# Layer two's list scheduler counts the SBUF port that VectorE and GpSimd share, with the output rows due one hidden row later

## The chip, the cores and the metric

One core of one Trainium2 chip runs the whole program. The metric is device time in microseconds, the median of several executions. One further execution was taken by the hardware profiler; all rows below are from it. PE is TensorE, DVE is VectorE, ACT is ScalarE, POOL is GpSimd, SP is the queue that issues most DMAs.

## The reference

Eight batches of eight-head Nystrom attention feed two feed-forward layers, all in fp32.

```python
x = attn_out.transpose(0, 2, 1, 3).reshape(B * S, H * D)   # 4608 x 512
a = x @ w1;  b = x @ w2
y = (a * b) @ w3 @ w_out                                   # layer one
h = y @ w_in                                               # 512 -> 2048
g = np.where(h > 0, h, np.exp(np.minimum(h, 0)) - 1)
out = g @ w_out2                                           # 2048 -> 512
```

## The kernel before

Attention and layer one fill the first part of the span. Every fp32 matrix is split into a high part (cast to fp32r) and a low part (source minus high), and each product is three matmuls: high by high, high by low, low by high.

**Layer two** works on transposed data in five blocks of 768, 1024, 1024, 1024 and 768 tokens. A block is cut into two halves (384 or 512 columns). For each block `i` and each of eight pairs `p` of 128-wide hidden slices there is a unit `u`, forty in all. A unit forms its 2x2 block product with seven multiplications in place of eight: `h_row` (L946) is one of them, a **hidden row** of six matmuls into one of two PSUM banks `h0`, `h1`, taken in turn. `h_put` (L969) empties the bank into the SBUF tile `g`: rows 0, 2, 3 and 6 are copied by ACT (L974), rows 1, 4 and 5 are added to what is there by DVE (L976: one operand in PSUM, one in SBUF). The next hidden row but one writes the same bank, so PE waits for the put.

After a half's puts come the ELU steps: ACT forms `m` and `t` (L987, L991, L995), DVE multiplies (`t<-m,t`, L999) and takes the maximum (`g<-t,g`, L1003), both with two operands in SBUF. POOL then forms four sums of quarters of `g` (`sums_g`, L1011), ACT casts the seven sources to high parts `eh` (L1022) and DVE subtracts to get the low parts `el` (`el<-g,eh` or `el<-tt,eh`, L1027, again two SBUF operands). Two units share one set of **output rows** (`o_row`, L1035): seven products for each of two halves `c`, six matmuls each, into the banks `o0` to `o5`. Five of the seven use the banks `o0` and `o1` in turn and are emptied by `o_put` (L1052) into `oa`: by ACT for a block's first units, else by DVE (L1059, one operand in PSUM).

At a block change POOL forms the sums of the next block's input (`sums_y`, `tv` and `yin`, L923), ACT casts the high parts (L933) and DVE subtracts the low parts (`yb`, L937, two SBUF operands). The weights arrive by DMA: `wh` per unit on POOL's queue (L891), `wp` per output row on SP's (L896).

**What sets the order.** From the step "2" of `STEPS` on, nothing is written in order by hand. `task` (L1075) records each step with its engine, a cost in ns, a latency and its dependences. `nominal` (L1232) writes one sequence of the PE rows: hidden rows first (`EARLY` of them beyond the second unit's seven), then two output rows and two hidden rows in turn. From it each PE row gets a due time, and `order` (L1251) computes backwards how late each step may start (`late`). It then plays the engines forward: whenever an engine is free it takes, of the steps that are ready, the one with the smallest `late` (L1301) and blocks the engine for its cost. The order in which steps were taken is the program order of every engine. On the chip each engine then works through its own list strictly in that order. The costs are

```python
def act_ns(n): return 87 + n / 1.2
def dve_ns(n, both=True): return (62 + n / 0.96) * (1.15 if both else 1.0)
def pool_ns(n): return 110 + 2.3 * n
```

so a DVE step with two SBUF operands (`both`) is charged 15% more, at all times alike.

Of the kernel before, what the change touches and what calls it, by code (L numbers as in the profile page):

```python
# [19 lines left out]
B, H, S, D = 8, 8, 576, 64  # L20
# [108 lines left out]
EARLY = 4  # L129
# [5 lines left out]
def nystrom_moe_kernel(ctx, tc, qT, kT, vm, vr, w12, w3T, w_out1, w_in2, w_out2, out):  # L135
# [524 lines left out]
    with tc.manual_schedule():  # L660
# [284 lines left out]

        def h_row(u, r):  # L946
            k, _ = H_ROWS[r]
            o, w = h_bank(u, r), wh[u]
            bh, bl = yb[u // NPAIR, k]
            first = r in (0, 1, 3)  # L950
# [18 lines left out]
        def h_put(u, r):  # L969
            o = h_bank(u, r)  # L970
            j, a = ((0, 0), (0, 0), (1, 0), (0, 1), (0, 1), (1, 0), (1, 1))[r]
            d = h_tile(u, j)[:, a, :]
            if r in (0, 2, 3, 6):
# [60 lines left out]

        def o_row(e, j, c):  # L1035
            k, p = O_ROWS[j], units2[e][1]
            o, w = o_bank(e, k, c), wp[e, j]
            first, cs = k in (0, 3, 5) or (p == 0 and k in (2, 6)), slice(c * 128, (c + 1) * 128)
# [13 lines left out]
        def o_put(e, j, c):  # L1052
            i, p = units2[e]
            k = O_ROWS[j]
            d, o = o_acc(i, O_ACC[k], c), o_bank(e, k, c)
            if p == 0 and k != 1:
                act.copy(d, o)
            else:
                dve.tensor_tensor(d, o, d, op=ALU.add)  # L1059
# [21 lines left out]
        def dve_ns(n, both=True):  # L1081
            return (62 + n / 0.96) * (1.15 if both else 1.0)
# [4 lines left out]
        def row_ns(n, k=6):  # L1087
            return k * (n + 33) / 2.4

        def first_layer(tail):  # L1090
            y0 = min(int(t[1:]) for t in tail if t[0] == "Y")
            for t in tail:
# [13 lines left out]
                elif c == "J":  # L1106
                    k = int(x)
                    task(("YL", 0, k), lambda k=k: part_lo(0, k), "DVE", dve_ns(768), 200, [("YH", 0, k)])
                elif c == ":":
                    task(t, lambda t=t: do(t), "DVE", 1200, 200)  # L1110
                else:
# [5 lines left out]
                    elif c == "g":  # L1117
                        task(("g", u), lambda u=u: ab_product(u), "DVE", dve_ns(NH, False), 150, [("G", u)])
                    elif c == "D":
                        task(("D", u), lambda u=u: ab_high(u), "ACT", act_ns(NH), 200, [("g", u), ("Y", u - 3)])  # L1120
                    elif c == "d":
                        task(("d", u), lambda u=u: ab_low(u), "DVE", dve_ns(NH), 150, [("D", u)])
# [11 lines left out]
        def second_layer():  # L1134
            prev = {}
            for u in range(n2):
# [4 lines left out]
                if p == 0 and i:  # L1141
                    for r in range(7):
# [3 lines left out]
                        task(("YL", i, k), lambda i=i, k=k: part_lo(i, k), "DVE", dve_ns(2 * n), 150, [("YH", i, k)])  # L1146
                for r in range(7):
                    b = (u + r) % 2
                    task(("R", u, r), lambda u=u, r=r: h_row(u, r), "PE", row_ns(n), 250, [("LW", u), ("YL", i, H_ROWS[r][0]), prev.get(b, "")], "H")
                    j = (0, 0, 1, 0, 0, 1, 1)[r]  # L1150
                    deps = [("R", u, r)]
                    if r == 0:
# [3 lines left out]
                    if r in (1, 4, 5):  # L1156
                        deps.append(("P", u, {1: 0, 4: 3, 5: 2}[r]))
                        task(("P", u, r), lambda u=u, r=r: h_put(u, r), "DVE", dve_ns(n, False), 150, deps)
# [3 lines left out]
                for j in range(2):  # L1162
# [8 lines left out]
                    task(("x", u, j), lambda u=u, j=j: elu_mul(u, j), "DVE", dve_ns(2 * n), 150, [("e", u, j)])  # L1171
                    task(("M", u, j), lambda u=u, j=j: elu_max(u, j), "DVE", dve_ns(2 * n), 150, [("x", u, j)])
# [15 lines left out]
        def out_tasks(e):  # L1188
            i, p = units2[e]
            n = width(e)  # L1190
            for j in range(7):
# [8 lines left out]
                for d in range(2):  # L1200
                    task(("GH", e, d, j), lambda e=e, d=d, j=j: g_hi(e, d, j), "ACT", act_ns(n), 200, [src(e + d), "p2"] + [("OR", *q[0], c) for c in range(2)])
                    task(("GL", e, d, j), lambda e=e, d=d, j=j: g_lo(e, d, j), "DVE", dve_ns(n), 150, [("GH", e, d, j)])
                for c in range(2):
# [3 lines left out]
                    if k in O_ACC:  # L1207
# [4 lines left out]
                    if k in O_ACC:  # L1212
# [4 lines left out]
                        else:  # L1217
                            w += [("OP", e - 2, j, c), ("OP", e, 0, c) if k == 1 else ""]
                            task(("OP", e, j, c), lambda e=e, j=j, c=c: o_put(e, j, c), "DVE", dve_ns(n, False), 150, w)
                        rot[c] = ("OP", e, j, c)  # L1220
            if p == NPAIR - 2:
                for q, w in ((0, [1, 2]), (1, [0, 3, 5]), (2, [4, 5]), (3, [6])):
                    for c in range(2):
# [3 lines left out]
                        task(("OE", i, q, c), lambda i=i, q=q, c=c: o_end(i, q, c), "DVE", dve_ns(n, q in (1, 2)), 150, w2)  # L1227
# [4 lines left out]
        def nominal():  # L1232
# [13 lines left out]
            while h or o:  # L1246
                seq += o[:2] + h[:2]
                o, h = o[2:], h[2:]
            return seq

        def order():  # L1251
# [26 lines left out]
            heap, out = [], []  # L1278
# [4 lines left out]
            while len(out) < len(names):  # L1283
                while heap and heap[0][0] <= t:
# [6 lines left out]
                    else:  # L1291
                        ready[tasks[k][1]].append(k)
                for e in free:
# [6 lines left out]
                    if c:  # L1300
                        k = min(c, key=lambda k: (late[k], rank[k]))  # L1301
# [4 lines left out]
                        free[e] = t + tasks[k][2]  # L1306
                        heapq.heappush(heap, (free[e] + tasks[k][3], len(names) + rank[k], ("done", k)))
# [75 lines left out]
```

## Time and profile before

| | |
|---|---|
| median of 3 runs | 1355.21 us (1353.44 to 1355.66) |
| the profiled execution | 1350.51 us |
| its span, first to last instruction | 1348.7 us (1.8 us lie around it) |
| busy: DVE, ACT, POOL | 1078.6, 793.8, 586.8 us |
| mean granted TensorE clock | 0.994 |

Busy time is the union of an engine's instructions. A matmul's record is longer than the step to the next one, so a wait shows in the idle column only by what it exceeds this overlap. The granted clock is 1.0 at 2.4 GHz and 0.5 at 1.2 GHz. Windows are stretches in us from the span's start. In the list of waits the releaser is the instruction whose end let the waiting one go. An instruction that is held up inside the engine, by a shared resource and not by a semaphore, shows as a longer duration of its own.

### The profile page before, as it was taken

The numbers are of one execution on the slowest core, as the hardware profiler recorded it, in microseconds if no ns is written. First come the engines' busy times: TensorE is split into PE (matmuls) and PEld (weight loads), VectorE is DVE, ScalarE is ACT, GpSimd is POOL, SyncE is SP. The second block draws the span as 40 slices with busy tenths as digits, with TensorE's granted clock in tenths as the row PEclk, the third lists the DMA queues.
The fourth block names the chain that finished last, engine by engine and source line by source line (L and its number), as shares of the span: only waits on it lengthen the run. The fifth ranks groups of instructions, "written<-read, shape, count | busy, mean of one in ns | idle before, by whom it ended". The sixth has DMA issues, their size and how long they took to land.

```text
span 1348.7 us, 24476 instructions
## 1 busy us (share of the span) xinstructions
PE 1302.9 (97%) x9456; PEld 1099.0 (81%) x9456; DVE 1078.6 (80%) x1680; ACT 793.8 (59%) x1433; POOL 586.8 (44%) x511
## 2 busy tenths in 40 slices
PE   5999999999999999989999899999999999999998
PEld 2458888888898889889999778886788777888997
DVE  7988767685868685663889978898789987899788
ACT  6675444454454454454768566765668577675763
POOL 5544245634572647221543534336334543334332
PEclk9999999999999999989999999999999999999999
DMA  9865445645675353423868564576555665457764
GB/s 344 317 210 172 138 152 190 235 169 164 214 249 193 130 207 136 181 94 135 329 231 296 211 224 158 196 268 206 200 206 181 232 238 187 170 209 257 264 228 156
DMA packets 81587, 279.19 MB, mean 207 GB/s; under 512 B 7232, under 2 KB 32832, under 8 KB 73280
## 3 DMA queue, kind: packets, MB, share of 16 engines
q1 hardware_dynamic: 75712, 204.24, 43.8%
q0 software_dynamic: 5760, 73.40, 15.1%
q8 instruction: 74, 1.21, 0.4%
q14 instruction: 41, 0.34, 0.1%
HBM read 229.38 MB, written 48.23 MB: 206 GB/s over the span
## 4 chain that ended last, share of the span: by engine, by line
PE 38%; DVE 18%; ACT 4%; issue 3%; DMA 1%; DVEq 0%; ACTq 0%; SPq 0%
DVE el L1027 6%; PE h L954 5%; PE h L956 5%; PE h L955 5%; PE o L1041 5%; PE o L1043 5%; PE o L1042 5%; DVE t L999 3%; DVE g L1003 2%; DVE g L976 2%; DVE oa L1059 2%; DVE yb L937 2%; PE y L847 1%; ACT eh L1022 1%; PE ab L812 1%
## 5 line engine op out<-in xcount | busy, mean ns | idle before, releaser
L954 PE MATMUL h<-yb,wh 128*128 128x512 f32 (+1 forms) x560 | 208.8, 373 | 11.5 <-DVE g L976 8.3
L955 PE MATMUL h<-yb,wh 128*128 128x512 f32 (+1 forms) x560 | 207.8, 371 | 4.1 <-DVE yb L937 4.1
L1041 PE MATMUL o<-eh,wp 128*128 128x512 f32 (+1 forms) x560 | 208.3, 372 | 3.2 <-DVE oa L1059 2.7
L1042 PE MATMUL o<-el,wp 128*128 128x512 f32 (+1 forms) x560 | 208.0, 371 | 0.8 <-DVE el L1027 0.8
L956 PE MATMUL h<-yb,wh 128*128 128x512 f32 (+1 forms) x560 | 208.5, 372 | 0.0
L1043 PE MATMUL o<-eh,wp 128*128 128x512 f32 (+1 forms) x560 | 208.2, 372 | 0.0
L1011 POOL TENSOR_TENSOR tt<-g,tt 128x512 f32<-128x512 f32 (+1 forms) x80 | 118.3, 1479 | 117.3 <-DVE el L1027 114.5
L1011 POOL TENSOR_TENSOR tt<-g,g 128x512 f32<-128x512 f32 (+1 forms) x40 | 54.6, 1364 | 252.6 <-DVE g L1003 217.2
L812 PE MATMUL ab<-ath,mh 128*128 128x288 f32 x512 | 158.1, 309 | 3.3 <-DVE a L825 3.3
L847 PE MATMUL y<-gh,w3oh 128*128 128x288 f32 x512 | 156.5, 306 | 0.1
L848 PE MATMUL y<-gl,w3oh 128*128 128x288 f32 x512 | 151.7, 296 | 2.4 <-DVE gl L836 2.4
L813 PE MATMUL ab<-atl,mh 128*128 128x288 f32 x512 | 151.8, 297 | 0.0
L849 PE MATMUL y<-gh,w3ol 128*128 128x288 f32 x512 | 151.3, 296 | 0.0
L814 PE MATMUL ab<-ath,ml 128*128 128x288 f32 x512 | 151.3, 295 | 0.0
L1027 DVE TENSOR_TENSOR el<-g,eh 128x512 fp32r<-128x512 f32 (+1 forms) x160 | 123.7, 792 | 27.2 <-ACT eh L1022 26.3
L987 ACT ACTIVATE m<-g 128x1024 f32<-128x1024 f32 (+1 forms) x80 | 78.2, 977 | 108.9 <-DVE g L976 73.6
L1027 DVE TENSOR_TENSOR el<-tt,eh 128x512 fp32r<-128x512 f32 (+1 forms) x120 | 118.9, 998 | 18.3 <-ACT eh L1022 17.6
L954 PEld LDWEIGHTS h<-yb,wh 128*128 128x128 f32 x560 | 105.3, 188 | 32.5 <-DVE g L976 13.7
L1041 PEld LDWEIGHTS o<-eh,wp 128*128 128x128 f32 x560 | 105.6, 188 | 23.4 <-DVE oa L1059 7.0
L955 PEld LDWEIGHTS h<-yb,wh 128*128 128x128 f32 x560 | 105.3, 188 | 19.2 <-DVE yb L937 4.7
L1042 PEld LDWEIGHTS o<-el,wp 128*128 128x128 f32 x560 | 105.7, 189 | 16.8 <-DVE el L1027 1.7
L999 DVE SCALAR_TENSOR_TENSOR t<-m,t 128x1024 f32<-128x1024 f32 (+1 forms) x80 | 95.2, 1190 | 29.9 <-ACT m L995 29.7
(154 smaller groups left out, 3066.4 us busy)
## 6 DMA issues: line engine op xcount, KB each, us to landing
wh<-wh_d POOLq DMA_DIRECT2D x40, 1792.0 KB, 8.2
wp<-wo_d SPq DMA_DIRECT2D x140, 512.0 KB, 3.6
wo_raw<-in_w_out_dram SPq DMA_DIRECT2D x24, 512.0 KB, 5.5
q<-in_qT_dram SPq DMA_DIRECT2D x8, 1152.0 KB, 6.4
k<-in_kT_dram SPq DMA_DIRECT2D x8, 1152.0 KB, 6.5
yd<-ysb SPq DMA_DIRECT2D x15, 576.0 KB, 3.6
w_raw<-in_w3T_dram SPq DMA_DIRECT2D x16, 512.0 KB, 5.7
w_raw<-in_w_dram SPq DMA_DIRECT2D x16, 512.0 KB, 5.0
```

Of the source, the lines that this page charges most:

```text
L812: pe.matmul(p[:, :NH], mh[:, cs], ah[:, blk, :], start=(blk == 0), stop=False)
L813: pe.matmul(p[:, :NH], mh[:, cs], al[:, blk, :], start=False, stop=False)
L847: pe.matmul(a[oc][:, :NH], w3o_hi[fc][:, os_], gh, start=(fc == 0), stop=False)
L848: pe.matmul(a[oc][:, :NH], w3o_hi[fc][:, os_], gl, start=False, stop=False)
L954: pe.matmul(o, ah, bh[:, kk, :], start=first and kk == 0, stop=False, skip_group_check=True)
L955: pe.matmul(o, ah, bl[:, kk, :], start=False, stop=False, skip_group_check=True)
L956: pe.matmul(o, al, bh[:, kk, :], start=False, stop=(kk == 1), skip_group_check=True)
L1011: pool.tensor_tensor(o, a, b, op=ALU.subtract)
L1027: dve.tensor_tensor(lo, s[:, a], hi.bitcast(F32), op=ALU.subtract)
L1041: pe.matmul(o, w[:, d, 0, cs], eh, start=first and d == 0, stop=False, skip_group_check=True)
L1042: pe.matmul(o, w[:, d, 0, cs], el, start=False, stop=False, skip_group_check=True)
L1043: pe.matmul(o, w[:, d, 1, cs], eh, start=False, stop=(d == 1), skip_group_check=True)
```

## The change

The 15% goes away. DVE steps with two SBUF operands become tasks of a class of their own, `"SBUF"`, still on DVE. The scheduler keeps a time `lock`: an `"SBUF"` step and a POOL sum each hold it from their start to 83 ns past their end, and one that starts while the other holds it is charged the rest of that hold less 130 ns. The same charge is added to a candidate's `late` when the scheduler picks, so that a step that would be held yields to one that would not. POOL's weight loads (`LW`) are exempt. `LATE_Y` gives the first block's `yb` subtractions a latency of 1200 in place of 200 ns. `EARLY` goes from 4 to 5. `SEEDED` is empty and `h_seeded` returns False, so every branch on them does what it did. No instruction is added, removed or resized.

```diff
-EARLY = 4
+EARLY = 5
+SEEDED = ()
+PATTERN = ((2, 2),)
+LATE_Y = 1200
...
-        def dve_ns(n, both=True):
-            return (62 + n / 0.96) * (1.15 if both else 1.0)
+        def dve_ns(n):
+            return 62 + n / 0.96
...
-                    task(("YL", 0, k), lambda k=k: part_lo(0, k), "DVE", dve_ns(768), 200, [("YH", 0, k)])
+                    task(("YL", 0, k), lambda k=k: part_lo(0, k), "SBUF", dve_ns(768), LATE_Y, [("YH", 0, k)])
...
-                    task(("x", u, j), lambda u=u, j=j: elu_mul(u, j), "DVE", dve_ns(2 * n), 150, [("e", u, j)])
-                    task(("M", u, j), lambda u=u, j=j: elu_max(u, j), "DVE", dve_ns(2 * n), 150, [("x", u, j)])
+                    task(("x", u, j), lambda u=u, j=j: elu_mul(u, j), "SBUF", dve_ns(2 * n), 150, [("e", u, j)])
+                    task(("M", u, j), lambda u=u, j=j: elu_max(u, j), "SBUF", dve_ns(2 * n), 150, [("x", u, j)])
...
-                    task(("GL", e, d, j), lambda e=e, d=d, j=j: g_lo(e, d, j), "DVE", dve_ns(n), 150, [("GH", e, d, j)])
+                    task(("GL", e, d, j), lambda e=e, d=d, j=j: g_lo(e, d, j), "SBUF", dve_ns(n), 150, [("GH", e, d, j)])
...
             while h or o:
-                seq += o[:2] + h[:2]
-                o, h = o[2:], h[2:]
+                for a, b in PATTERN:
+                    seq += o[:a] + h[:b]
+                    o, h = o[a:], h[b:]
...
-            heap, out = [], []
+            heap, out, lock = [], [], 0.0
...
-                        ready[tasks[k][1]].append(k)
+                        ready["DVE" if tasks[k][1] == "SBUF" else tasks[k][1]].append(k)
...
-                        k = min(c, key=lambda k: (late[k], rank[k]))
+                        held = {"SBUF": max(0, lock - t - 130), "POOL": max(0, lock - t - 130) if e == "POOL" else 0}
+                        k = min(c, key=lambda k: (late[k] + held.get(tasks[k][1], 0), rank[k]))
...
                         free[e] = t + tasks[k][2]
+                        if tasks[k][1] == "SBUF" or (e == "POOL" and k[0] != "LW"):
+                            free[e] += held[tasks[k][1]]
+                            lock = free[e] + 83
```

The later `yb` (`YL`), layer one's `d` steps and two of the four final sums (`OE`) become `"SBUF"` in the same way.

**What moves.** The lists of all engines are the same up to PE's second hidden row; everything after is the same instructions in another order. In the rows below, numbers within a name are the unit and the part (`g90`: unit 9, half 0; `el66`: unit 6, output row 6; `wp6_4`: output row 4 of units 6 and 7), the number after the last underline is a buffer's. Lines of the changed kernel are 3 to 15 higher.

First place: DVE's list at the start of layer two, where PE runs the last rows of layer one (`ab`, and `y` from `gh` and `gl`) between the first hidden rows. Before:

```order
L836 TENSOR_TENSOR gl116_8101<-a116_8054,gh116_8092 128x288
L937 TENSOR_TENSOR yb102_8096<-yin0_7987,yb002_8095 128x2x384
L937 TENSOR_TENSOR yb105_8099<-yin0_7987,yb005_8098 128x2x384
L937 TENSOR_TENSOR yb103_8120<-tv00_8076,yb003_8119 128x2x384
L825 TENSOR_TENSOR a117_8131<-ab117_1_8111,a117_8131 128x288
L937 TENSOR_TENSOR yb101_8135<-tv01_8077,yb001_8134 128x2x384
L836 TENSOR_TENSOR gl117_8168<-a117_8131,gh117_8162 128x288
L976 TENSOR_TENSOR g00_8144<-h1_8124,g00_8144 128x384
```

With the change:

```order
L839 TENSOR_TENSOR gl116_8119<-a116_8054,gh116_8092 128x288
L828 TENSOR_TENSOR a117_8121<-ab117_1_8108,a117_8121 128x288
L940 TENSOR_TENSOR yb102_8096<-yin0_7987,yb002_8095 128x2x384
L839 TENSOR_TENSOR gl117_8171<-a117_8121,gh117_8151 128x288
L828 TENSOR_TENSOR a118_8173<-ab118_1_8144,a118_8173 128x288
L940 TENSOR_TENSOR yb101_8132<-tv01_8077,yb001_8131 128x2x384
L839 TENSOR_TENSOR gl118_8202<-a118_8173,gh118_8200 128x288
L940 TENSOR_TENSOR yb103_8117<-tv00_8076,yb003_8116 128x2x384
L984 TENSOR_TENSOR g00_8153<-h1_8124,g00_8153 128x384
```

The product `a117`, for which PE's next `ab` rows wait, stood behind three `yb` subtractions and now stands ahead of all but the first; `yb105` and `yb103` went back. On PE the 24 matmuls of `ab118` and of one `y` step now stand between the first hidden row and the second, which needs `yb102`.

Second place: DVE's list at the change from block 0 to block 1, around the put of unit 9's hidden row 4 (`g90<-h1`). Before:

```order
L999 SCALAR_TENSOR_TENSOR t81_9816<-m81_9815,t81_9816 128x1024
L1059 TENSOR_TENSOR oa10_8647<-o0_8747,oa10_8647 128x384
L1059 TENSOR_TENSOR oa11_8648<-o1_8748,oa11_8648 128x384
L1003 TENSOR_TENSOR g81_9699<-t81_9816,g81_9699 128x1024
L1027 TENSOR_TENSOR el66_9876<-tt6_9582,eh66_9875 128x384
L1027 TENSOR_TENSOR el76_9891<-tt7_9754,eh76_9890 128x384
L976 TENSOR_TENSOR g90_9806<-h1_8124,g90_9806 128x512
L1059 TENSOR_TENSOR oa20_8937<-o0_8747,oa20_8937 128x384
L1059 TENSOR_TENSOR oa21_8951<-o1_8748,oa21_8951 128x384
```

With the change:

```order
L1074 TENSOR_TENSOR oa20_8949<-o0_8741,oa20_8949 128x384
L1007 SCALAR_TENSOR_TENSOR t81_9844<-m81_9843,t81_9844 128x1024
L984 TENSOR_TENSOR g90_9794<-h1_8124,g90_9794 128x512
L1074 TENSOR_TENSOR oa21_8961<-o1_8742,oa21_8961 128x384
L984 TENSOR_TENSOR g91_9880<-h0_8123,g91_9880 128x512
L1011 TENSOR_TENSOR g81_9664<-t81_9844,g81_9664 128x1024
L1035 TENSOR_TENSOR el66_9893<-tt6_9623,eh66_9892 128x384
L1035 TENSOR_TENSOR el76_9935<-tt7_9779,eh76_9934 128x384
L984 TENSOR_TENSOR g100_9954<-h1_8124,g100_9954 128x512
```

The put stood behind a maximum and two low parts (all with two SBUF operands). Now this put and the next (`g91<-h0`) stand ahead of those three, which follow them.

Third place: PE's list at the same block change, between output rows 3 and 4 of units 6 and 7. Before:

```order
L1043 MATMUL o1_8748<-eh73_9788,wp6_3_9687 128x384
L954 MATMUL h0_8123<-yb013_9557,wh9_9620 128x512
L955 MATMUL h0_8123<-yb113_9558,wh9_9620 128x512
L956 MATMUL h0_8123<-yb013_9557,wh9_9620 128x512
L954 MATMUL h0_8123<-yb013_9557,wh9_9620 128x512
L955 MATMUL h0_8123<-yb113_9558,wh9_9620 128x512
L956 MATMUL h0_8123<-yb013_9557,wh9_9620 128x512
L954 MATMUL h1_8124<-yb014_9568,wh9_9620 128x512
L955 MATMUL h1_8124<-yb114_9569,wh9_9620 128x512
L956 MATMUL h1_8124<-yb014_9568,wh9_9620 128x512
L954 MATMUL h1_8124<-yb014_9568,wh9_9620 128x512
L955 MATMUL h1_8124<-yb114_9569,wh9_9620 128x512
```

With the change:

```order
L1058 MATMUL o0_8741<-eh73_9805,wp6_3_9686 128x384
L1056 MATMUL o1_8742<-eh63_9730,wp6_3_9686 128x384
L1057 MATMUL o1_8742<-el63_9731,wp6_3_9686 128x384
L1058 MATMUL o1_8742<-eh63_9730,wp6_3_9686 128x384
L1056 MATMUL o1_8742<-eh73_9805,wp6_3_9686 128x384
L1057 MATMUL o1_8742<-el73_9806,wp6_3_9686 128x384
L1058 MATMUL o1_8742<-eh73_9805,wp6_3_9686 128x384
L1056 MATMUL o0_8741<-eh64_9773,wp6_4_9733 128x384
L1057 MATMUL o0_8741<-el64_9774,wp6_4_9733 128x384
```

Two hidden rows stood between `o1` of output row 3 and `o0` of output row 4; now `o0` of row 4 follows at once. Groups of three or more output rows on end, the final eighteen left out, were one before and are ten now. Ahead of the first output row stand 19 hidden rows, before 20.

## Rows read from the trace of the kernel before

**Rows 1.** The page, part 1: busy time of the matmul engine over the span.
```profile
PE 1302.9 (97%) x9456; PEld 1099.0 (81%) x9456; DVE 1078.6 (80%) x1680; ACT 793.8 (59%) x1433; POOL 586.8 (44%) x511
```

**Rows 2.** Windows, PE alone: stretch, its length, PE busy (matmuls), granted clock, DMA share, GB/s.
```profile
577.00:587.00 10.00, 6.51 (x30) 0.66 0.19 67
631.10:690.00 58.90, 56.66 (x316) 1.00 0.83 305
748.00:768.04 20.04, 16.66 (x74) 0.91 0.54 193
768.04:800.00 31.96, 30.35 (x129) 1.00 0.58 196
800.00:910.00 110.00, 110.00 (x477) 1.00 0.61 212
910.00:960.00 50.00, 46.57 (x198) 1.00 0.59 204
1072.00:1084.00 12.00, 10.14 (x42) 1.00 0.25 81
1226.00:1232.00 6.00, 5.50 (x26) 1.00 0.50 173
1250.00:1327.00 77.00, 77.00 (x443) 1.00 0.65 229
1327.00:1344.60 17.60, 15.59 (x77) 1.00 0.45 154
```

**Rows 3.** Windows of the matmuls that write tile h (hidden rows) alone.
```profile
577.00:587.00 10.00, 2.75 (x10) 0.66 0.19 67
748.00:768.04 20.04, 9.17 (x36) 0.91 0.54 193
1226.00:1232.00 6.00, 2.61 (x14) 1.00 0.50 173
```

**Rows 4.** Waits of PE, 577 us to the end: us in total, times, longest.
```profile
PE h L954 <- DVE g L976: 8.3, 9, 2.7
...
PE h L954 <- ACT g L974: 2.9, 4, 1.3
PE o L1041 <- DVE oa L1059: 2.7, 7, 0.7
```

**Rows 5.** Lines by form, DVE, 600 to 1349 us: xcount | busy, mean ns | idle before.
```profile
L1027 DVE TENSOR_TENSOR el<-tt,eh 128x512 fp32r<-128x512 f32 x72 | 78.8, 1104 | 13.1 <-ACT eh L1022 13.1
...
L976 DVE TENSOR_TENSOR g<-h,g 128x512 f32<-128x512 f32 x72 | 49.0, 682 | 3.2 <-PE h L956 2.1 <-ACT g L974 0.5
...
L1059 DVE TENSOR_TENSOR oa<-o,oa 128x384 f32<-128x384 f32 x64 | 33.5, 545 | 1.8 <-PE o L1043 1.6
```

**Rows 6.** Lines by form, POOL, 570 to 1349 us, same columns.
```profile
L923 POOL TENSOR_TENSOR tv<-yin,tv 128x1024 f32<-128x1024 f32 x6 | 16.4, 2733 | 0.1
```

**Rows 7.** Timeline, all engines, 752 to 763 us: start, us, instruction [idle <-releaser].
```profile
752.08 3.44 DVE L1003 TENSOR_TENSOR g<-t,g 128x1024 f32<-128x1024 f32 x1
...
755.45 2.08 DVE L1027 TENSOR_TENSOR el<-tt,eh 128x384 fp32r<-128x384 f32 x2
...
757.45 0.68 DVE L976 TENSOR_TENSOR g<-h,g 128x512 f32<-128x512 f32 x1
...
758.18 0.50 PE L954 MATMUL h<-yb,wh 128*128 128x512 f32 x1 [2.69 <-DVE g L976]
...
759.73 0.52 PE L1041 MATMUL o<-eh,wp 128*128 128x384 f32 x1
...
760.04 0.52 PE L1042 MATMUL o<-el,wp 128*128 128x384 f32 x1
...
762.10 4.19 DVE L999 SCALAR_TENSOR_TENSOR t<-m,t 128x1024 f32<-128x1024 f32 x1
```

**Rows 8.** Timeline, all engines, 578 to 581 us.
```profile
578.34 5.05 DVE L937 TENSOR_TENSOR yb<-yin,yb 128x768 fp32r<-128x768 f32 x2
...
580.96 0.69 PE L955 MATMUL h<-yb,wh 128*128 128x384 f32 x1 [3.17 <-DVE yb L937]
```

More of the change, by code (lines that the diff above doesn't have):

```diff
@@ L944, in h_bank, with h_seeded @@
             return banks[(u + r) % 2][:, : width(u)]
+        def h_seeded(u):
+            return False
         def h_row(u, r):
@@ L949, in h_row @@
             bh, bl = yb[u // NPAIR, k]
-            first = r in (0, 1, 3)
+            first = r in (0, 3) or (r == 1 and not h_seeded(u))
             for kk in range(2):
@@ L972, in h_put @@
             d = h_tile(u, j)[:, a, :]
-            if r in (0, 2, 3, 6):
+            if r == 0 and h_seeded(u):
+                act.copy(h_bank(u, 1), o)
+            elif r in (0, 2, 3, 6) or (r == 1 and h_seeded(u)):
                 act.copy(d, o)
@@ L1033, in o_bank, with o_seeded, o_seed @@
             return obanks[2 * {2: 1, 6: 2}.get(k, 0) + c][:, : width(e)]
+        def o_seeded(p, k):
+            return p > 0 and k in SEEDED
+        def o_seed(e, j, c):
+            k = O_ROWS[j]
+            act.copy(o_bank(e, k, c), o_acc(units2[e][0], O_ACC[k], c))
         def o_row(e, j, c):
@@ L1037, in o_row @@
             o, w = o_bank(e, k, c), wp[e, j]
-            first, cs = k in (0, 3, 5) or (p == 0 and k in (2, 6)), slice(c * 128, (c + 1) * 128)
+            first, cs = k == 0 or (k in (3, 5) and not o_seeded(p, k)) or (p == 0 and k in (2, 6)), slice(c * 128, (c + 1) * 128)
             for d in range(2):
@@ L1055, in o_put @@
             d, o = o_acc(i, O_ACC[k], c), o_bank(e, k, c)
-            if p == 0 and k != 1:
+            if (p == 0 and k != 1) or o_seeded(p, k):
                 act.copy(d, o)
@@ L1117, in first_layer @@
                     elif c == "g":
-                        task(("g", u), lambda u=u: ab_product(u), "DVE", dve_ns(NH, False), 150, [("G", u)])
+                        task(("g", u), lambda u=u: ab_product(u), "DVE", dve_ns(NH), 150, [("G", u)])
                     elif c == "D":
@@ L1121, in first_layer @@
                     elif c == "d":
-                        task(("d", u), lambda u=u: ab_low(u), "DVE", dve_ns(NH), 150, [("D", u)])
+                        task(("d", u), lambda u=u: ab_low(u), "SBUF", dve_ns(NH), 150, [("D", u)])
                     elif c == "Y":
@@ L1155, in second_layer @@
                         deps += [("GL", e, d, jj) for e, d in [((u - 3) // 2 * 2, (u - 3) % 2)] for jj in (2, 4)] + [("S", u - 3, 3), *(["p2"] if u else [("YL", 0, k) for k in (0, 2, 4, 5)])]
-                    if r in (1, 4, 5):
+                    if r in (4, 5) or (r == 1 and not h_seeded(u)):
                         deps.append(("P", u, {1: 0, 4: 3, 5: 2}[r]))
-                        task(("P", u, r), lambda u=u, r=r: h_put(u, r), "DVE", dve_ns(n, False), 150, deps)
+                        task(("P", u, r), lambda u=u, r=r: h_put(u, r), "DVE", dve_ns(n), 150, deps)
                     else:
@@ L1206, in out_tasks @@
                         w += [("C", len(units) - 1, oc) for oc in range(KD)] + [("g", len(units) - 1)]
-                    if k in O_ACC:
+                    if o_seeded(p, k):
+                        f = [rot[c], ("OP", e - 2, j, c), ("OP", e - 2, 3, c) if k == 5 else ""]
+                        task(("OS", e, j, c), lambda e=e, j=j, c=c: o_seed(e, j, c), "ACT", act_ns(n), 200, f)
+                        w.append(("OS", e, j, c))
+                    elif k in O_ACC:
                         w.append(rot.get(c, ""))
@@ L1218, in out_tasks @@
                             w += [("OP", e - 2, j, c), ("OP", e, 0, c) if k == 1 else ""]
-                            task(("OP", e, j, c), lambda e=e, j=j, c=c: o_put(e, j, c), "DVE", dve_ns(n, False), 150, w)
+                            if o_seeded(p, k):
+                                task(("OP", e, j, c), lambda e=e, j=j, c=c: o_put(e, j, c), "ACT", act_ns(n), 200, w)
+                            else:
+                                task(("OP", e, j, c), lambda e=e, j=j, c=c: o_put(e, j, c), "DVE", dve_ns(n), 150, w)
                         rot[c] = ("OP", e, j, c)
@@ L1226, in out_tasks @@
                             w2.append(("OE", i, q - 1, c) if q > 1 else "")
-                        task(("OE", i, q, c), lambda i=i, q=q, c=c: o_end(i, q, c), "DVE", dve_ns(n, q in (1, 2)), 150, w2)
+                        task(("OE", i, q, c), lambda i=i, q=q, c=c: o_end(i, q, c), "SBUF" if q in (1, 2) else "DVE", dve_ns(n), 150, w2)
                         task(("OO", i, q, c), lambda i=i, q=q, c=c: o_out(i, q, c), "SP", 60, 4000, [("OE", i, q, c)])
```

8 lines of the change are left out of this document (5 added, 3 removed).

## The prediction

> **What bounds the kernel now.** I read the page's busy table first, then stretches of PE, then PE's waits, then the two engines behind those waits, and last the timeline at the longest waits. The busy table says that PE works 97% of the span [rows 1], so an instruction that becomes cheaper elsewhere gains nothing by itself; only time in which PE stands or runs slowly can be won. The change reorders nothing before 577 us, so the rest of the span is all that matters.
>
> The stretches [rows 2] show where PE loses time, if one counts matmuls in place of busy time. In the quiet stretch from 800 to 910 us 477 matmuls of 512 columns take 110 us, 0.2306 each; from 1250 to 1327 us 443 of 384 columns take 77 us, 0.1738 each; one of 288 columns I scale to 0.130. At this pace the other stretches need, and so lose:
> - 577 to 587 (start of layer two): 10 hidden matmuls of 384 [rows 3] and 20 of 288 need 4.4 of 10 us, **5.6** lost;
> - 631 to 690 (first pairs): 316 of 384 need 54.9 of 58.9, **4.0** lost;
> - 748 to 768 (change to block 1): 36 hidden of 512 [rows 3] and 38 output matmuls of 384 need 14.9 of 20.0, 5.1 lost; 768 to 800: 129 of 512 need 29.7 of 32.0, 2.2 lost; together **7.3**;
> - 910 to 960 (block 2): 198 of 512 need 45.7 of 50, **4.3** lost; 1072 to 1084 (block 3): 42 need 9.7 of 12, **2.3** lost; 1226 to 1232 (block 4): 14 hidden of 384 [rows 3] and 12 of 512 need 5.2 of 6, **0.8** lost;
> - 1327 to the last matmul: 77 of 384 need 13.4 of 17.6, **4.2** lost.
>
> That is 28.5 us, all that a better order could win. Outside these stretches layer two runs at its pace.
>
> The waits say what for [rows 4]: hidden rows wait for the put of their bank, 8.3 us on DVE and 2.9 us on ACT; output rows wait 2.7 us on DVE's put. The put itself is quick: 682 ns with one operand in PSUM, against a mean of 1104 ns for a subtraction of the same size with both in SBUF [rows 5]. The timeline shows the difference as one event [rows 7]: `g<-t,g` takes 3.44 us and a pair of 384-wide `el` 2.08 us, then the put takes its 0.68 and PE, idle for 2.69 us, starts 0.05 us after it. `t<-m,t` of the same width as `g<-t,g` takes 4.19 us soon after. POOL's long input sums, mean 2733 ns [rows 6], run at these places, so I read the stretched instructions as DVE waiting for POOL's hold on a shared port. At 577 us it is the same: two `yb` take 5.05 us and PE waits 3.17 us for the first [rows 8]. After this wait and after the one of 2.69 us the granted clock was lower, 0.66 and 0.91 on average over their stretches [rows 2], which is full speed mixed with the half-speed level of 1.2 GHz; 384-wide matmuls then start 0.31 us apart [rows 7].
>
> **The change, part by part.** Nothing is added or removed; the sum is a list of PE waits that go, stay or come.
>
> Start. The first long wait is for `yb102` [rows 8]. In the new lists 24 matmuls of 288 columns come first, 24 x 0.130 = 3.1 us of work, as long as the wait; and `a117` no longer stands behind three subtractions. Next late is `a118`, behind `yb102` and `gl117`, either of which can be held by an input sum; I leave 1.4 us of the 5.6 there, no slow clock, and gain **4.2**. Bounds: 2.0, if one wait of that length stays and brings the slow clock, and 5.6.
>
> First pairs. The waits for puts sit behind stretched subtractions as above; the two earliest, near 631 and 634 us, follow from ACT's and PE's own order in a place that the change hardly alters. I leave 1.4 of 4.0: gain **2.6**, bounds 1 and 4.
>
> Block changes. The second place of the order lists is the wait of 2.69 us itself: the put now stands ahead of the three instructions that kept it waiting 3.44 + 2.08 us. The held instructions move behind two puts, so their users come later: `el66` and `el76` feed the last output row of units 6 and 7, and `g81` the POOL sums. PE has hidden rows to go on with there. So the waits for hidden banks go, and with the wait of 2.69 us the slow clock after it: 11 matmuls at 0.31 for 0.174, 1.5 us, which lie within the 5.1 above.
>
> What comes instead is the third place. With two output rows on end, the put of `o0` must be done in the time of the `o1` row between, 6 x 0.1738 = 1.04 us. The put alone takes 0.545 [rows 5], so it makes it when DVE is free; behind one unheld `g<-t,g` or `t<-m,t`, which I take at 1.2 us (twice the put's columns, at 0.68 us for half of them [rows 5]), it is 0.7 late, and with one `el` more 1.3. Ten such groups exist. I charge 1.5 us in each of the changes to blocks 1, 2 and 3, where held instructions are longest, and nothing in the other seven. The four changes lose 7.3 + 4.3 + 2.3 + 0.8 = 14.7 us now; with 4.5 us for these waits and 0.1 at block 4 the gain is **10.1**. Bounds: 5.6, if every charge doubles, and 14.7.
>
> The end. No hidden rows are left to fill PE, and the waits for output puts stay. The new list has two of the final additions (545 ns each) behind puts for which PE waits, not ahead: gain **1.1** of 4.2, bounds 0 and 1.1.
>
> DMAs. `wp` and `wh` issues move with their rows. The waits of PE that weigh from 577 us on are on engines [rows 4], and the loads run a ring ahead. Cost nothing; if a load came late, PE would show a wait on it.
>
> The sum is 4.2 + 2.6 + 10.1 + 1.1 = **18.0 us**. The profiled execution took 1350.5 us, so the changed one would take 1332.5. The median of the runs shown lies 4.7 us above the profiled execution, for a reason that no row gives; I keep that offset: 1355.2 - 18.0 = **1337.2 us**. No change means within 0.2%, 2.7 us.
>
> **The rivals.**
>
> Half the gain (chance 0.10). The new waits on output puts grow past 2 us and the slow clock returns at one or two of them, 1.5 us each as at 760 us. Then about 9 us are won: 1346. Speaking for it: a wait of 2.69 us was enough [rows 7]. The Trainium skill, TensorE: Matmul & The Clock Gate, Part 1, holds that the array is throttled unless it is kept active; the two drops here agree, and by it every longer stall is paid for twice.
>
> The order fits only its own clock (0.04, no change). Without the 15% there is no slack; if the modelled hold and the real one drift apart, the charge falls on the wrong step. A wait of 0.9 us, about twice what the mean held `el` exceeds a free put by (0.42 [rows 5]), in each of the 20 unit pairs would eat 18 us: 1355. Against it: a charge at the model's wrong place is still rarer than none, and the steady stretches hold DVE's delays without any PE wait now.
>
> The exclusion isn't what stretches these instructions (0.02, no change). Then the reordering is arbitrary: 1355. Rows 5 speak against it: with one operand in PSUM the mean stays at 682. The Trainium skill, Advanced Engine Details and Errata, VectorE Performance Modes, names only two-port modes as interfering with GpSimd. By that note alone the new charge has no subject and the sum would be 0; the rows of this case carry more weight.
>
> Slower (0.04). The groups of output rows on end become the bound: each of the ten meets a held instruction. The worst held one, 4.19 us [rows 7], with the put's 0.545 less the 1.04 of cover is 3.7 us, and the slow clock adds 1.5: 5.2 each, 52 for ten less 4.5 charged, so 1385 at the worst. It decides from 2.5 us on average in ten places (25 against the 4.5 charged): then the 18.0 are gone and 2.7 more. For a middle case of 3 us, 1337.2 + 25.5 = 1363. Against it: the scheduler sees these waits in its own play, with the holds in it.
>
> **How the numbers follow.** The forecast has 0.80. Its bounds: the gains at their best 5.6 + 4 + 14.7 + 1.1 = 25.4, so 1330, and the runs' offset may shrink with the waits, so I go to 1329. At their least 2 + 1 + 5.6 + 0 = 8.6, so 1346.6; this also holds the half-gain rival, and I end at 1346. Faster by over 0.2%: 0.80 + 0.10 = 0.90; within: 0.04 + 0.02 = 0.06; slower: 0.04.
>
> **What would show it.** Right: PE's waits for hidden banks on DVE fall from 8.3 us to under 2; the window from 577 to 587 us holds over 50 matmuls, now 30, and no clock under 1.0; the new waits are on output puts, each under 2.2 us; DVE's puts keep 0.68 us, and `t<-m,t` near a block change may still take 3 us with nobody waiting. Wrong: a wait of PE on `el` or on a DMA, or half speed after an output put. The mean of `el<-tt,eh` need not fall: the holds are moved to where they hurt less, not avoided. The prediction fails in kind if the hidden-bank waits stay.

## The result, and the profile after

The changed kernel takes **1332.20 us** (median of 4 runs, 1330.67 to 1333.91); the kernel before, in the same comparison, 1355.25 us (1353.44 to 1355.66). The ratio is 0.9834, 95% interval 0.9818 to 0.9849: 23.0 us, or 1.7%, faster. Forecast were 1337.2 us in a range of 1329 to 1346, and faster with a chance of 0.90.

| | before | after |
|---|---|---|
| median of the runs | 1355.25 us | 1332.20 us |
| the profiled execution | 1350.51 us | 1330.83 us |
| its span | 1348.7 us | 1329.1 us |
| mean granted TensorE clock | 0.994 | 0.998 |

The busy row of the page, after, answers to [rows 1]. DVE and POOL work as long as before (DVE 1078.5 us against 1078.6); PE's busy time is 8.6 us less; the half-speed matmuls of [rows 2] and [rows 7] are gone.

```profile
PE 1294.3 (97%) x9456; PEld 1097.0 (83%) x9456; DVE 1078.5 (81%) x1680; ACT 798.1 (60%) x1433; POOL 586.7 (44%) x511
```

Windows of the changed kernel, PE alone, with the columns of [rows 2]. Layer two starts at 577 us in both; later stretches lie earlier now.

```profile
577.00:587.00 10.00, 9.63 (x61) 1.00 0.21 76
626.90:685.80 58.90, 57.83 (x323) 1.00 0.83 305
736.00:764.00 28.00, 25.84 (x126) 1.00 0.72 263
764.00:800.00 36.00, 36.00 (x157) 1.00 0.67 232
890.00:940.00 50.00, 49.89 (x217) 1.00 0.68 242
1050.00:1070.00 20.00, 19.92 (x87) 1.00 0.50 169
1205.00:1222.00 17.00, 17.00 (x85) 1.00 0.67 229
1308.00:1324.40 16.40, 14.89 (x78) 1.00 0.47 155
```

The same for the matmuls of hidden rows alone, with the columns of [rows 3]:

```profile
577.00:587.00 10.00, 3.46 (x17) 1.00 0.21 76
736.00:764.00 28.00, 15.63 (x66) 1.00 0.72 263
```

At the pace of the prediction (0.2306, 0.1738 and 0.130 us a matmul of 512, 384 and 288 columns) these stretches lose:

| stretch | lost before | left, forecast | left, measured | working |
|---|---|---|---|---|
| start, 577 to 587 | 5.6 | 1.4 | 1.3 | 17 x 0.1738 + 44 x 0.130 = 8.7 of 10 |
| first pairs, 626.9 to 685.8 | 4.0 | 1.4 | 2.8 | 323 x 0.1738 = 56.1 of 58.9 |
| to block 1, 736 to 800 | 7.3 | 1.5 | 2.3 | 66 x 0.2306 + 60 x 0.1738 = 25.7 of 28; the rest is full |
| to blocks 2, 3, 4 | 7.4 | 3.1 | 0 | 217 x 0.2306 = 50.0 of 50; 87 x 0.2306 = 20.1 of 20; busy 17.00 of 17 |
| end, from 1308 | 4.2 | 3.1 | 2.8 | 78 x 0.1738 = 13.6 of 16.4 |
| sum | 28.5 | 10.5 | 9.2 | gain 19.3, forecast 18.0 |

The first pairs are taken 4.2 us earlier than before, as layer two is ahead by that much. The gain of 19.3 us found in these stretches agrees with the 19.7 us by which the two profiled executions differ.

PE's waits from 577 us to the end answer to [rows 4] (total, times, longest, in us):

```profile
PE o L1056 <- DVE oa L1074: 2.5, 4, 1.5
PE o L1057 <- DVE el L1035: 1.1, 2, 0.7
PE h L961 <- DVE yb L940: 1.0, 1, 1.0
PE h L960 <- DVE g L984: 1.0, 3, 0.4
PE h L960 <- ACT g L982: 0.8, 2, 0.6
```

The wait of hidden rows for DVE's put fell from 8.3 to 1.0 us, that for ACT's from 2.9 to 0.8. The largest left is on output puts, 2.5 us in four waits, longest 1.5; before it was 2.7 us in seven. DVE by form, 600 us to the end, with the columns of [rows 5]:

```profile
L1035 DVE TENSOR_TENSOR el<-tt,eh 128x512 fp32r<-128x512 f32 x72 | 69.0, 974 | 2.0 <-ACT eh L1030 2.0
...
L984 DVE TENSOR_TENSOR g<-h,g 128x512 f32<-128x512 f32 x72 | 49.2, 685 | 9.9 <-PE h L962 7.9 <-ACT yb L936 0.6
...
L1074 DVE TENSOR_TENSOR oa<-o,oa 128x384 f32<-128x384 f32 x64 | 34.8, 550 | 5.1 <-PE o L1058 4.9
```

The puts take what they took. This subtraction with two SBUF operands fell from 1104 to 974 ns on average, but other such forms rose: `yb<-tv,yb` of 1024 columns from 1403 to 1647 ns, `el<-tt,eh` of 384 columns from 840 to 916. With DVE's busy time as long as before, its holds (what POOL adds to the length of DVE's steps) were moved and in total not avoided.

### The profile page after: what moved, and what is told of

The parts are those of the page before. It is cut to its first block, busy times and chain, and to the rows that moved or that the text cites. A ratio compares the mean times of both kernels' runs of the same rounds, so it can differ in the third digit from the quotient of the medians.

```text
span 1329.1 us, 24431 instructions
## 1 busy us (share of the span) xinstructions
PE 1294.3 (97%) x9456; PEld 1097.0 (83%) x9456; DVE 1078.5 (81%) x1680; ACT 798.1 (60%) x1433; POOL 586.7 (44%) x511
## 4 chain that ended last, share of the span: by engine, by line
PE 50%; DVE 7%; ACT 3%; DMA 2%; issue 1%; POOL 0%; DVEq 0%; ACTq 0%; SPq 0%; POOLq 0%
PE h L962 7%; PE h L960 7%; PE h L961 7%; PE o L1057 7%; PE o L1058 7%; PE o L1056 7%; DVE el L1035 3%; PE y L850 1%; PE ab L815 1%; PE y L851 1%; PE y L852 1%; DVE g L1011 1%; PE ab L816 1%; PE ab L817 1%; DVE oa L1074 1%
## 5 line engine op out<-in xcount | busy, mean ns | idle before, releaser
L982 ACT COPY g<-h 128x512 f32<-128x512 f32 (+1 forms) x160 | 86.2, 540 | 69.2 <-PE h L962 52.7
L960 PEld LDWEIGHTS h<-yb,wh 128*128 128x128 f32 x560 | 105.1, 188 | 18.8 <-DVE g L984 2.2
L815 PEld LDWEIGHTS ab<-ath,mh 128*128 128x128 f32 x512 | 96.5, 188 | 27.8 <-issue 15.2
L1007 DVE SCALAR_TENSOR_TENSOR t<-m,t 128x1024 f32<-128x1024 f32 (+1 forms) x80 | 98.1, 1227 | 25.3 <-ACT m L1003 25.0
```

The costliest lines, as they stand in the source:

```text
L815: pe.matmul(p[:, :NH], mh[:, cs], ah[:, blk, :], start=(blk == 0), stop=False)
```

## The experiments

Each tells what it alters. "Before" is the kernel before in the same comparison: 1356.18 us for the first four runs, 1355.74 for the next four, 1356.90 for the next three, 1356.47 for the last.

**1. No lock.** The scheduler neither charges a hold nor the 15%.

```diff
-                            lock = free[e] + 83
+                            lock = 0.0
```

> The changed kernel with the port's hold taken out of the scheduler (lock stays 0); the 15% is gone too, EARLY 5 and LATE_Y 1200 stay. Theory A (the charge for the hold is what moves held instructions behind the puts): no step is charged for holds at all, so hidden rows wait for puts on DVE by at least the 8.3 us of before, and the time is 1350 us or more. Rival B1 (the gain comes from the cheaper, truer DVE costs): 1332 us, within 3. Rival B2 (it comes from the later output row and LATE_Y): below 1340 us.

Measured: 1383.54 us (1382.28 to 1386.52), ratio 1.0214 (1.0188 to 1.0239). The rest of the change is worth nothing without the lock; with no charge at all the kernel is slower than before by 27 us. The expectation put the loss on DVE's puts, 8.3 us or more; PE waits 4.3 us for those. Its largest wait is on ACT's:

```profile
PE h L960 <- ACT g L982: 25.9, 9, 6.3
```

The timeline of all engines around the longest of these nine waits shows the chain behind it:

```profile
913.85 2.40 POOL L926 TENSOR_TENSOR tv<-yin,tv 128x1024 f32<-128x1024 f32 x1
...
914.39 7.10 DVE L1035 TENSOR_TENSOR el<-tt,eh 128x512 fp32r<-128x512 f32 x1
...
916.20 2.40 POOL L926 TENSOR_TENSOR yin<-yin 128x1024 f32<-128x1024 f32 x1
...
918.56 2.37 POOL L926 TENSOR_TENSOR tv<-yin,tv 128x1024 f32<-128x1024 f32 x1
...
921.41 1.21 DVE L1007 SCALAR_TENSOR_TENSOR t<-m,t 128x1024 f32<-128x1024 f32 x1
...
922.72 1.06 ACT L995 ACTIVATE m<-g 128x1024 f32<-128x1024 f32 x1 [8.95 <-DVE t L1007]
...
926.60 0.79 PE L960 MATMUL h<-yb,wh 128*128 128x512 f32 x1 [6.25 <-ACT g L982]
```

A low part that needs 0.68 us takes 7.10, over three input sums that POOL runs one after the other, at 2.4 us each less than their mean in [rows 6]. `t<-m,t` stands behind it, ACT's `m<-g` waits 8.95 us for that, ACT's put stands behind `m<-g`, and PE waits 6.25 us for the put. So this wait of PE on ACT came from a hold on DVE. The other eight were not followed.

**2. A flat 15%, with the other edits.** The lock is off and the old factor is back where the engines are played forward (the backward count of `late`, which had it before, stays without it); `EARLY` = 5 and `LATE_Y` = 1200 stay.

```diff
-                        free[e] = t + tasks[k][2]
+                        free[e] = t + tasks[k][2] * (1.15 if tasks[k][1] == "SBUF" else 1.0)
...
-                            lock = free[e] + 83
+                            lock = 0.0
```

> As e1_no_lock, but DVE steps with two SBUF operands are charged 15% more again, as before the change: what is left of the change is EARLY 5 and LATE_Y 1200. Theory A: waits for puts on DVE above 5 us, time 1345 to 1355 us. Rival B2 (later output row and LATE_Y): 1332 us, within 3.

Measured: 1357.06 us (1354.73 to 1360.37), ratio 1.0015 (1.0000 to 1.0029). The two numbers without the lock bring nothing. The window at the start of layer two (columns as in [rows 2]) is as bad as before:

```profile
577.00:587.00 10.00, 6.51 (x27) 0.66 0.15 50
```

In this kernel the mean of `el<-tt,eh` 128x512 is 979 ns, in the changed one 974, and they lie 25 us apart. All of DVE's work takes 1085.8 us here, 7 us more; but it took as long in the kernel before as in the changed one, 23 us apart. So it is not the total of the holds that counts but which steps they hit.

**3. `EARLY` back to 4.**

```diff
-EARLY = 5
+EARLY = 4
```

> The changed kernel with EARLY back at 4, so the hold and LATE_Y alone. Theory A: nearly all of the gain stays, 1331 to 1338 us; the hidden rows' waits on DVE puts stay under 3 us. Rival B2 (one more hidden row of cover is what removes them): above 1343 us, and these waits back at 6 us or more.

Measured: 1339.45 us (1337.18 to 1342.91), ratio 0.9894 (0.9864 to 0.9923). The lock (with `LATE_Y`) brings about 14 of the 22 us that the ratios give, `EARLY` = 5 the other 8. That is less than the theory asked, and more than its rival: hidden rows wait 4.4 us for DVE's puts here, 1.0 in the changed kernel, 8.3 before. The start is mended without it: 55 matmuls from 577 to 587 us, at full clock.

**4. Before, without the port.** The order of before; each of POOL's sums becomes a fill.

```diff
-            pool.tensor_tensor(o, a, b, op=ALU.subtract)
+            pool.memset(o, 0.0)
```

> The kernel before, its order unchanged, with every sum of layer two on GpSimd (sums_g and sums_y) replaced by a memset of the same destination, which reads no SBUF; the sums of the Winograd scheme are left out. If a port shared with GpSimd's reads stretches DVE's instructions: the mean of el<-tt,eh of 512 columns falls from 1104 to under 720 ns, hidden rows' waits on DVE puts fall from 8.3 to under 3 us, and the old order alone takes 1328 to 1338 us (up to 28.5 us less than before, some of it because a memset may be shorter than a sum). If something in DVE's own list is slow: the mean stays above 1000 ns and the time stays within 5 us of 1355.

Measured: 1325.19 us (1323.38 to 1327.14), ratio 0.9780 (0.9756 to 0.9804). 31 us go without any reordering. But a fill of 512 columns takes POOL 530 ns, and the sum is then ready sooner; the next run takes that apart.

**5. The same, with POOL kept as slow.**

```diff
-            pool.tensor_tensor(o, a, b, op=ALU.subtract)
+            pool.tensor_tensor(o[:, :8], a[:, :8], b[:, :8], op=ALU.subtract)
+            pool.memset(o, 0.0)
+            pool.memset(o, 0.0)
```

> The kernel before, in its own order; each of GpSimd's sums (input sums and sums of g) now subtracts only 8 columns, which keeps its dependences, and then fills its target twice with a constant, which keeps it about as long as a sum that is not held up (two fills of 525 ns against 1.29 us). So it leaves out the Winograd sums, as the run with one fill did. That run also made GpSimd's steps less than half as long, so it could have gained from their earlier results and not from the free port. Port: GpSimd as slow as before and VectorE still never held, 1325 to 1333 us, and subtractions of 512 columns with two SBUF operands at 0.68 us. Rival, the earlier results did it: at least 10 of the 31 us come back, 1335 us or more.

Measured: 1328.41 us (1322.18 to 1329.09), ratio 0.9791 (0.9766 to 0.9817), the same as run 4 within the intervals. Lines by form of POOL, 600 us to the end:

```profile
L1015 POOL MEMSET tt<- 128x512 f32 x72 | 38.0, 527 | 4.1
L1014 POOL MEMSET tt<- 128x512 f32 x72 | 37.9, 526 | 4.3
L1013 POOL TENSOR_TENSOR tt<-g,tt 128x8 f32<-128x8 f32 x80 | 34.1, 426 | 84.7 <-DVE el L1031 81.8
```

The three make 1.48 us for one sum. Lines by form of DVE, same stretch:

```profile
L1001 DVE SCALAR_TENSOR_TENSOR t<-m,t 128x1024 f32<-128x1024 f32 x48 | 58.5, 1220 | 9.3 <-ACT m L997 9.3
...
L1031 DVE TENSOR_TENSOR el<-tt,eh 128x512 fp32r<-128x512 f32 x72 | 48.6, 685 | 14.4 <-ACT eh L1026 14.4
```

DVE's subtraction is at 685 ns on average, over all 72, and `t<-m,t` at 1.22 us, the 1.2 that the prediction took for one that isn't held, while POOL takes nearly as long as with its sums (562.3 us busy, before 586.8). DVE is busy for 992.2 us in place of 1078.6, so its holds come to some 86 us. PE's waits from 577 us on come to 3.4 us, of them 0.7 for DVE's puts. The constants in the fills don't make PE faster: from 800 to 890 us it does 392 matmuls, as in the changed kernel. So the cause is shown to be that POOL's sums read SBUF, not how long they take. The Trainium skill (SBUF — State Buffer, Who interferes with whom) says that a VectorE instruction with two SBUF inputs contends with a GpSimd instruction that reads SBUF and not with one that only writes it; this run agrees, 1104 ns against 685.

**6. After, without the port,** with the replacement of run 5 in the changed kernel.

> The changed kernel, its own order, with the same replacement of GpSimd's sums (leaves the Winograd sums out). If the new order does nothing but move held steps away from PE's waits, it has nothing to win once nothing is held: as fast as the old order with the same replacement, within 3 us, 1323 to 1333 us. Rival, the order is better in itself (output rows later, or two on end): then it beats the old order with the same replacement by 5 us or more. If the runs of output rows on end cost something of their own, it is slower than the old order by 1 to 4 us.

Measured: 1324.33 us (1323.40 to 1324.85), ratio 0.9771 (0.9754 to 0.9787). The medians of runs 5 and 6 lie 4.1 us apart, but the intervals overlap: in itself the new order shows no gain clear of the noise. Most of its 23 us come from putting the holds where PE doesn't wait for them. Between its ratio and the 0.9834 of the changed kernel lie some 8 us that the holds still cost.

**7. The charge without the yielding.** The pick goes by `late` alone.

```diff
-                        k = min(c, key=lambda k: (late[k] + held.get(tasks[k][1], 0), rank[k]))
+                        k = min(c, key=lambda k: (late[k], rank[k]))
```

> The changed kernel, but the pick goes by late alone, without the charge; what is picked is still charged its hold, so the clock of the scheduler stays right. The change has two parts here: a clock that knows the holds, and a pick that lets a step yield when it would be held. Theory, the clock does it: 1331 to 1336 us, within 4 us of the changed kernel. Rival, the yielding does it: half of the 23 us are lost or more, 1343 to 1356 us.

Measured: 1335.99 us, median of three executions (1334.67 to 1337.66), ratio 0.9858 (0.9839 to 0.9877); a fourth, which took 2674.59 us, is not counted. Of the gain about 20 us stay; that the yielding brings the other 3 is not shown, as the intervals overlap.

**8. `LATE_Y` back to 200.**

```diff
-LATE_Y = 1200
+LATE_Y = 200
```

> The changed kernel with the latency of the first block's low parts back at 200 ns. I gave the start of layer two 4.2 of the 18.0 us without telling which edit brings it. Theory, the lock alone does it: 1331 to 1335 us and still over 50 matmuls from 577 to 587 us. Rival, the latency of 1200 does it: the wait of some 3 us for yb and the half speed after it come back, 4 us more, 1335 to 1338 us, and about 30 matmuls in that stretch.

Measured: 1332.78 us (1332.20 to 1335.11), ratio 0.9837 (0.9821 to 0.9853): no difference to the changed kernel. The start holds 57 matmuls at full clock without it:

```profile
577.00:587.00 10.00, 9.22 (x57) 1.00 0.20 70
```

**9. The yielding without the charge.** A picked step is charged its bare length; only the end of the hold still counts the rest (the expectation calls the hold bare too, which the edit doesn't make it).

```diff
-                            free[e] += held[tasks[k][1]]
-                            lock = free[e] + 83
+                            lock = free[e] + held[tasks[k][1]] + 83
```

> The changed kernel with the other half alone: the pick still yields by the rest of a hold, but a held step is charged only its bare length, and so is the hold. The run without the yielding kept 19 of the 23 us. Theory, it is the clock that counts: without the charge the scheduler's time runs ahead of the chip's, and yielding on a wrong clock brings little: 1345 us or more, and possibly over the kernel before, as the run with no lock at all (1383.5). Rival, either half does it: 1340 us or less.

Measured: 1386.35 us (1385.41 to 1388.02), ratio 1.0212 (1.0197 to 1.0228), as with no lock at all. With runs 1 and 7 this settles which half acts: the clock that knows the holds. A pick that yields on a clock that does not gains nothing.

**10. Another mix of rows,** a candidate to beat both kernels.

```diff
-PATTERN = ((2, 2),)
+PATTERN = ((2, 1), (2, 3))
...
-            return 62 + n / 0.96
+            return (62 + n / 0.96) * 1
```

The second edit changes no cost.

> A candidate to beat both kernels: the changed kernel with PATTERN = ((2, 1), (2, 3)), two output rows, one hidden row, two output rows, three hidden rows. About 6 us lie between the changed kernel and the two orders without a held step, of them 1.6 us in one wait for an output put at 744 us and 0.9 us in one for a low part at 759 us, where output rows stand close. If these waits depend on how the rows are mixed, they go: 1327 to 1331 us. If the rest is spread over many small holds: 1331 to 1334 us. If the three hidden rows on end wait for their banks, as rows on end did in the kernel before: 1335 us or more.

Measured: 1339.41 us (1338.21 to 1341.90), ratio 0.9862 (0.9846 to 0.9879): slower than the changed kernel beside it (run 11) by about 3 us, with intervals that just overlap. PE's waits for output puts did shrink, from 2.5 to 1.3 us, but those for low parts rose from 1.1 to 3.7 us and those of hidden rows for DVE's puts from 1.0 to 4.4. The longest, in the timeline of all engines:

```profile
757.05 7.87 DVE L1035 TENSOR_TENSOR el<-tt,eh 128x384 fp32r<-128x384 f32 x2
...
758.41 1.30 POOL L1019 TENSOR_TENSOR tt<-g,g 128x512 f32<-128x512 f32 x1
...
759.66 2.41 POOL L926 TENSOR_TENSOR tv<-yin,tv 128x1024 f32<-128x1024 f32 x1
...
764.98 0.45 PE L1057 MATMUL o<-el,wp 128*128 128x384 f32 x1 [2.88 <-DVE el L1035]
```

Two low parts take 7.87 us beside POOL's sums, and PE waits 2.88 us for one of them.

**11. The changed kernel again.**

> The changed kernel once more, unaltered, beside the candidate. In the prediction the median of the runs lay 4.7 us above the profiled execution and I kept that offset; the changed kernel showed 1.4. If the offset belongs to a kernel, it is 1.4 us again here within 1 us, and the median stays at 1331 to 1334 us; if the profiled execution is one draw out of a spread of several us, the offset comes out otherwise, between -2 and 5 us, with the median in the same place.

Measured: 1336.12 us (1333.43 to 1337.28), ratio 0.9838 (0.9821 to 0.9855), 20.8 us under the kernel before: the same ratio as in the first comparison, though the median lies 2 us above the range expected. Its profiled execution took 1336.26 us, so the offset is -0.1 us. Its timeline at block 2 has a wait that the first profile of the same kernel has not (there PE idles 0.1 us in all from 890 to 940 us):

```profile
901.76 3.38 POOL L926 TENSOR_TENSOR tv<-yin,tv 128x1024 f32<-128x1024 f32 x1
...
902.81 2.87 DVE L1035 TENSOR_TENSOR el<-tt,eh 128x512 fp32r<-128x512 f32 x1
...
905.61 1.28 DVE L1074 TENSOR_TENSOR oa<-o,oa 128x512 f32<-128x512 f32 x2
...
906.34 0.50 PE L1056 MATMUL o<-eh,wp 128*128 128x512 f32 x1 [1.72 <-DVE oa L1074]
```

The output put stands behind a low part held for 2.87 us, and PE waits 1.72 us. Which step meets a hold varies between executions of one kernel.

**12. `EARLY` = 6,** the second candidate.

> The changed kernel with EARLY = 6. From 4 to 5 the median fell from 1339.5 to 1332.2 us (ratio to the kernel before 0.9894 to 0.9834). If a later first output row goes on giving the low parts room, a ratio of 0.978 to 0.982 and a kernel that beats both; if 5 had all there was, and the waits that are left stand behind ordinary steps of VectorE and not behind held ones, 0.982 to 0.985; if the output rows that are pushed back pile up at the block changes, 0.985 or more.

Measured: 1348.96 us (1346.87 to 1353.84), ratio 0.9951 (0.9935 to 0.9966). Nearly all is lost, and PE's waits are those of the kernel before again:

```profile
PE h L960 <- DVE g L984: 10.1, 8, 3.0
```

Of these 10.1 us, 7.0 lie at the changes to blocks 1, 2 and 3 (2.6, 3.0 and 1.4). So 4, 5 and 6 give 0.9894, 0.9834 and 0.9951: 5 is a best point of this list and no rule. Why 5 helps and 6 undoes it was not followed up. No run beats the changed kernel with its sums in place.

## Why the prediction was right, and where it was off

**Start: right, 1.3 us left against 1.4.** 61 matmuls in the stretch, over 50 were asked, and no clock under 1.0. The prediction didn't say which edit does it. Runs 2, 3 and 8 do: `LATE_Y` and `EARLY` with the flat 15% leave 27 matmuls at a clock of 0.66, the lock without `LATE_Y` or with `EARLY` = 4 gives 57 and 55. It is the lock.

**First pairs: half of the gain, 1.2 in place of 2.6 us.** The mis-sized term. Of the 4.0 us, 1.4 were to stay, from the two early waits; 2.8 stayed. The two early waits are there as forecast: PE's steps at 627.0 and 630.7 us take 0.86 and 0.68 us in place of 0.17, so 1.2 lost. Of the other 1.6 the largest piece, 0.6, is a wait that the kernel before doesn't have here:

```profile
632.04 0.96 DVE L1007 SCALAR_TENSOR_TENSOR t<-m,t 128x768 f32<-128x768 f32 x1 [0.93 <-ACT m L1003]
...
633.91 0.55 DVE L984 TENSOR_TENSOR g<-h,g 128x384 f32<-128x384 f32 x1
634.51 0.44 PE L960 MATMUL h<-yb,wh 128*128 128x384 f32 x1 [0.41 <-DVE g L984]
```

The put stands behind `t<-m,t` and `g<-t,g` (0.96 us each), and neither is held. The prediction took the waits for puts here to sit behind stretched steps alone; a charge for holds doesn't see this one.

**Block changes: mechanism right, the charge too high.** 2.3 us are left where 4.6 were charged, all of them at block 1. Hidden rows hardly wait any more, as forecast. The new waits were on output puts, as forecast, but one in place of three in this execution. That one went as priced. Timeline, all engines:

```profile
744.04 0.55 DVE L1035 TENSOR_TENSOR el<-tt,eh 128x384 fp32r<-128x384 f32 x1
...
744.51 1.21 DVE L1011 TENSOR_TENSOR g<-t,g 128x1024 f32<-128x1024 f32 x1
...
745.64 1.01 DVE L1074 TENSOR_TENSOR oa<-o,oa 128x384 f32<-128x384 f32 x2
...
746.25 0.45 PE L1056 MATMUL o<-eh,wp 128*128 128x384 f32 x1 [1.47 <-DVE oa L1074]
```

The put of `o0` stands behind an unheld `el` and an unheld `g<-t,g`, 1.3 us late by the prediction, and PE waits 1.47. At block 2 the wait came in run 11 (1.72 us) and not in the first profile, so a charge for two of the three would have been nearest. What the prediction named as a sign that it was wrong, a wait of PE on `el`, is there too, though small: 1.1 us in two waits. It was no good sign, as the kernel before has such waits as well:

```profile
PE o L1042 <- DVE el L1027: 0.8, 2, 0.4
```

The longer one after the change:

```profile
754.72 5.66 DVE L1035 TENSOR_TENSOR el<-tt,eh 128x384 fp32r<-128x384 f32 x2
754.74 2.42 POOL L926 TENSOR_TENSOR tv<-yin,tv 128x1024 f32<-128x1024 f32 x1
...
757.10 1.29 POOL L1019 TENSOR_TENSOR tt<-g,g 128x512 f32<-128x512 f32 x1
...
758.47 1.50 POOL L1019 TENSOR_TENSOR tt<-g,tt 128x512 f32<-128x512 f32 x1
...
760.43 0.45 PE L1057 MATMUL o<-el,wp 128*128 128x384 f32 x1 [0.69 <-DVE el L1035]
```

Two low parts of 384 columns take 5.66 us beside one input sum and two sums of `g`, and PE waits 0.69. This is what is left where a held step has no room to go to.

**The end: right**, 2.8 us left against 3.1.

**The sum: right, 19.3 against 18.0.** The forecast of the median was 5.0 us too high. Of these, 1.7 are the larger gain (19.7 between the two profiled executions), and 3.3 are **the offset of 4.7 us between the runs' median and the profiled execution, which was kept**. It fell to 1.4 us, and to -0.1 in run 11. It was no property of the kernel: the kernel before ran 38 times beside the experiments, from 1351.24 to 1360.63 us, and the profiled 1350.51 lies under all of them. That profile was a draw from the fast end. What the other executions lose more is open: they have no rows here, and the two profiles of the changed kernel show only that a wait like that of block 2 can come and go.

**The rivals.** Half the gain, through the slow clock at the new waits: it did not come here, the stretch from 736 to 764 us is at 1.00 with its wait of 1.47 us. Run 10 shows that it can:

```profile
759.00:769.00 10.00, 7.12 (x29) 0.83 0.66 246
904.00:912.00 8.00, 5.71 (x19) 0.79 0.10 37
```

There a wait of 2.88 us and one of 2.3 us are followed by half speed, a clock of 0.83 and 0.79 on average over these stretches, and the shorter waits of the changed kernel are not, as the prediction had it. The Trainium skill (TensorE: Matmul & The Clock Gate, Part 1), by which the array is throttled unless it is kept active, agrees with run 10. But not every longer stall is paid for twice, as the prediction read it: the last section has one of 3.05 us that is not. An order that fits only its own clock: runs 1 and 9 show how dear a clock is that runs ahead of the chip's (27 to 29 us), and run 7 that the charge keeps it near enough. The exclusion is not what stretches DVE: run 5 refutes this rival. Output rows on end as the new bound: run 6 has the same groups of them and is no slower than run 5, and in the changed kernel, with its holds, all waits for output puts come to 2.5 us.

## What to carry to other kernels

An average surcharge for a shared port spreads over all steps what hits a few (the kernels before and after have the same total of holds and lie 23 us apart), so let the scheduler's clock hold the exclusion where it happens; a rule about yielding added some 3 us to that, not clear of the noise. To price such a port before the work, replace what reads through it by fills of the same length: runs 5 and 6 so put the cost of the holds at 27 to 31 us, and reordering won 20 to 23. Take the gain from the stretches of one profile, but the base from several executions, since one profile can be the fastest of many.

## What the runs showed of the hardware that was not expected

A VectorE step that loses the port can lose it several times in a row: 7.10 us for a step of 0.68 over three sums on end in run 1, while none of POOL's three was stretched. The charge of the change (the rest of one hold) does not cover this.

After waits of PE of 2.88 and 2.3 us the granted clock fell in run 10. After one of 3.05 us in run 12 it did not; the window around it, PE alone:

```profile
903.00:910.00 7.00, 3.95 (x18) 1.00 0.22 84
```

So the length of a single wait did not decide it in these runs. What else did was not tried.
